# Layer 2 of a fused attention and two-layer kernel in units of 512 tokens instead of 384, with its buffers moved by 32 bytes

## The chip, the cores and the metric

The kernel runs on one core of one Trainium2 chip. The metric is the device time of one execution in microseconds (us). Three runs of the kernel before took 903.63, 903.86 and 904.91 us; the median is 903.86 us.

## The reference

Windowed attention over 4 x 8 heads, 576 positions and head size 64, then two layers over the 4 x 576 = 2304 tokens it leaves, each of width 512 with 2048 inner columns. Everything is fp32.

```python
def _moe_ref(x, w_in, w_out):          # layer 1
    h = np.maximum(x @ w_in, 0.0)
    return (h * h @ w_out)

def _moe2_ref(x, w_in, w_out):         # layer 2
    h = x @ w_in
    g = h * np.cos(h)
    return (g @ w_out)

x = attention(q, k, v)   # causal, window 64, softmax; regrouped to (2304, 512)
x = _moe_ref(x, ...)
return _moe2_ref(x, ...)
```

## The kernel before, in words

**Numbers.** Each fp32 operand of a layer's products is split into a high and a low fp32r part, and a product is three matmuls: high by high, and the two mixed ones. So one product of 128 contracted rows costs three LDWEIGHTS and three MATMULs.

**Work.** Both layers go through their tokens unit by unit, and within a unit through j = 0 to 15, 16 slices of 128 inner columns. One pair (unit, j) is called an item here. Its first product (function `g1`, matmuls at L833, tile `ph`) multiplies four 128-row chunks of w_in, the stationary operand, by the unit's X: 12 matmuls as wide as the unit has tokens. The activation follows on ScalarE (ACT) and VectorE (DVE). Its second product (`g2`) is added up over the 16 items in PSUM. In layer 1 (class `UnitA`, L624, tiles `accA`) w_out is stationary and the activations `g` move; units are 256 tokens three times and then 512 tokens three times, and the output goes through DRAM (`x2d`). In layer 2 (class `UnitB`, L766, tiles `accB`) the activations `gb` are stationary, 128 tokens at a time, and 512 columns of w_out move: three matmuls for each 128 tokens, whatever the unit's size. Layer 2 has six units of 384 tokens (`UB`), so an item is 12 matmuls of 384 columns and 9 of 512.

**Activation of layer 2** (`UnitB.act`): ACT `u` (L717), DVE rounding (L721), two DVE steps of range reduction (L725, L729) and a clamp (L732), ACT sine (L736), DVE product (L739), ACT copy to `gb` high (L743), DVE `gb` low (L746). All are as wide as the unit.

**Order.** A planner (`Plan.run`) writes out one list of instructions for each engine before anything runs. It goes by costs (`pe_us`, `act_us`, `dve_us`), by keys, and by rings that stand for the buffers; each engine then takes its list in that order. TensorE (PE) has a list laid down by `line`: in layer 2 `g1` of item i, then `g2` of item i-3.

**Buffers.** PSUM has four accumulators (`acc`), one for each 128 tokens of a layer-2 unit, and four tiles for `ph`. At a unit's end `UnitB.finish` copies each accumulator to one of the two `x2` tiles (L788, L790) and stores it (L794). The next unit's inputs come through the same two `x2` tiles (`UnitB.load`, L679, L683, L686). SBUF is filled from the left (X, the weights `W`, the layer-1 tiles `r`, `g`, `x2`) and, by pools opened with `side="right"`, from its right end: the attention's buffers, and after them the layer-2 pool `bp` with `u`, `r` and `gb`. In the built program every left-hand buffer named here starts at a multiple of 64 bytes (X at 17088, the weight slots from 49856 on, `g` at 193216 and 197312), and every buffer of the right end starts 32 bytes off one (`gb` at 217056, 220128, 223200, 226272; `qk` at 211296). The attention of the first two 256-token blocks is an exception: its second half (`guest`) lies in weight slots on the left.

Of the kernel before, what the change touches and what calls it, by code (L numbers as in the profile page):

```python
# [9 lines left out]
F32 = mybir.dt.float32  # L10
F32R = mybir.dt.float32r
# [17 lines left out]
def f32(ap):  # L29
    return ap.bitcast(F32)  # L30
# [55 lines left out]
class Plan:  # L86
# [80 lines left out]
def dve_us(n, fast=False):  # L167
    return 0.065 + n / (1920.0 if fast else 960.0)
# [4 lines left out]


def pe_us(n, passes=1):
    return max(0.107, 0.004 + passes * n / 2207.0)


@with_exitstack
def kernel(  # L180
# [53 lines left out]
    def dma(key, fn, nbytes, deps=(), take=(), use=(), n=1, order=()):  # L234
        return op({"SP": max(0.6 * n, nbytes / 360e3)}, key, fn, [*deps, *order], take, use, lat=2.2)
# [4 lines left out]
    def copy(e, o, i, scale=1.0):  # L240
        if e == "ACT":
            nc.scalar.activation(o, i, AF.Copy, scale=scale)  # L242
        elif e == "POOL":
            nc.gpsimd.tensor_scalar(o, i, scale, 1.0, ALU.mult, ALU.mult)
        elif scale == 1.0:
            nc.vector.tensor_copy(o, i)
        else:
            nc.vector.tensor_scalar(o, i, scale, None, ALU.mult)
# [408 lines left out]
                        x2_done[n, c] = o  # L657

    class UnitB:
        w = UB  # L660
        tiles = UB // P

        def __init__(self, n):
            self.n = n
            self.acc_b = [R["acc"].buf() for _ in range(self.tiles)]
            self.acc = {}
            self.xb = R["X"].buf()
            self.ready = {}

        def xt(self):  # L670
            return X[:, :, :, (2 * UA, 0)[self.xb.slot]:]

        def load(self, key, after, l=None):
            for c in range(NCC):
                t, b = {}, R["x2"].buf()

                def ld(e, c=c, t=t):
                    t["x"] = ma.tile([P, 512], F32, tag="x2", name=f"xr_{self.n}_{c}")
                    nc.sync.dma_start(  # L679
                        t["x"][:, 0:UB], x2d[:, c, self.n * UB:self.n * UB + UB])  # L680

                def hi(e, c=c, t=t):
                    copy(e, self.xt()[:, 0, c, 0:UB], t["x"][:, 0:UB])  # L683

                def lo(e, c=c, t=t):
                    nc.vector.tensor_tensor(  # L686
                        self.xt()[:, 1, c, 0:UB], t["x"][:, 0:UB], f32(self.xt()[:, 0, c, 0:UB]),
                        ALU.subtract)

                first, last = self.n * UB // UA, (self.n * UB + UB - 1) // UA  # L690
# [4 lines left out]
                l = dma(key + c, ld, P * UB * 4, deps, [b] + ([self.xb] if c == 0 else []),  # L695
                        [self.xb] if c else [])
                h = op({"DVE": dve_us(UB, True), "ACT": act_us(UB)}, key + c, hi, [l], use=[b, self.xb])
                o = op({"DVE": dve_us(UB)}, key + c, lo, [h], use=[b, self.xb])
                self.ready[c] = [h, o]
            return l  # L700

        def x(self, hl, c):
            return self.xt()[:, hl, c, 0:UB]

        def x_ready(self, c):
            return self.ready[c]
# [2 lines left out]
            return [self.xb]  # L709

        def act(self, ph, phb, nm, key, o_g1):
            ub, rb, gb = R["bu"].buf(), R["br"].buf(), R["bg"].buf()
            t = {}

            def e0(e):
                t["u"] = bp["b"].tile([P, UB], F32, tag="u", name=f"u_{nm}")
                nc.scalar.activation(  # L717
                    t["u"], ph()[:, 0:UB], AF.Identity, bias=quarter, scale=INV_2PI)

            def e1(e):  # L720
                nc.vector.tensor_scalar(t["u"], t["u"], MAGIC, MAGIC, ALU.add, ALU.subtract)  # L721

            def e2(e):
                t["r"] = bp["b"].tile([P, UB], F32, tag="r", name=f"rr_{nm}")
                nc.vector.scalar_tensor_tensor(  # L725
                    t["r"], t["u"], -C1, ph()[:, 0:UB], ALU.mult, ALU.add)

            def e3(e):
                nc.vector.scalar_tensor_tensor(t["r"], t["u"], -C2, t["r"], ALU.mult, ALU.add)  # L729

            def e4(e):
                nc.vector.tensor_scalar(  # L732
                    t["r"], t["r"], -PI_IN - HALF_PI, PI_IN - HALF_PI, ALU.max, ALU.min)

            def e5(e):
                nc.scalar.activation(t["u"], t["r"], AF.Sin, bias=hpi)  # L736

            def e6(e):
                nc.vector.tensor_tensor(t["r"], ph()[:, 0:UB], t["u"], ALU.mult)  # L739
# [8 lines left out]
            o = op({"ACT": act_us(UB, False)}, key, e0, [o_g1] + open_b, [ub], [phb])  # L748
            if sines:
                sines[-1].deps.append(o)  # L750
            o = op({"DVE": dve_us(UB, True)}, key, e1, [o], use=[ub])
            o = op({"DVE": dve_us(UB)}, key, e2, [o], [rb], [ub, phb])
            o = op({"DVE": dve_us(UB)}, key, e3, [o], use=[ub, rb])
            o = op({"DVE": dve_us(UB, True)}, key, e4, [o], use=[rb])
            o = op({"ACT": act_us(UB) + 0.1}, key, e5, [o], use=[ub, rb])
            sines.append(o)
            o = op({"DVE": dve_us(UB)}, key, e6, [o], use=[ub, rb, phb])
            h = op({"ACT": act_us(UB)}, key, e7, [o], [gb], [rb])
            l = op({"DVE": dve_us(UB)}, key, e8, [h], use=[rb, gb])
            return t, gb, [h, l]  # L760

        def g2(self, j, m, t, w):
# [7 lines left out]
        groups = UB // P  # L770
        group_us = 3 * pe_us(DM)

        def g2_bufs(self, j, m):
# [2 lines left out]
        def finish(self, key, o_last):  # L776
            for i in range(self.tiles):
                extra = self.n == NUB - 1 and i == self.tiles - 1
                t, b = {}, R["bg" if extra else "x2"].buf()

                def cp_(e, i=i, t=t, extra=extra):
                    if extra:
                        t["o"] = bp["b"].tile(
                            [P, 2 * UB], F32, tag="g", bufs=4, name=f"o_{self.n}_{i}")[:, 0:DM]
                    else:
                        t["o"] = ma.tile([P, DM], F32, tag="x2", name=f"o_{self.n}_{i}")
                    if e == "ACT":
                        nc.scalar.activation(t["o"], self.acc[i], AF.Copy)  # L788
                    else:
                        nc.vector.tensor_copy(t["o"], self.acc[i])  # L790

                def st(e, i=i, t=t):
                    r0 = self.n * UB + i * P
# [86 lines left out]
    for i in range(len(items) + LAG + 1):  # L880
# [95 lines left out]
```

## Time and profile before

| | |
|---|---|
| median of three runs | 903.86 us |
| the profiled execution | 904.37 us |
| its span, first to last instruction | 902.6 us |
| mean granted TensorE clock | 0.992 |
| PE busy | 879.0 us, 97% of the span |
| DVE busy / ACT busy | 563.3 us, 62% / 480.2 us, 53% |
| layer 2's products, first start to last | 489.58 us to 898.7 us |

The profile is of one execution, 0.51 us above the median of the runs. Its "busy" time of PE counts a matmul from its start to its modelled end; neighbouring matmuls overlap in it. The time that a matmul really takes from the stream is the distance from its start to the next one's start. In the timeline, the first column of a row is the start of a run of like instructions, the second the time from there to the end of the last of them.

### The profile page before, as it was taken

What the parts mean: (1) busy time and instruction counts of PE and PEld (TensorE: products, weight loads), DVE (VectorE), ACT (ScalarE), POOL (GpSimd) and SP (SyncE); (2) the same over time, 40 slices, a digit from 0 to 9 for tenths busy, and PEclk for the clock granted to TensorE, in tenths of its full rate; (3) what the DMA queues carried; (4) which work ended last, traced back from release to release, by engine and by line L of the source; (5) the groups of instructions that cost most, each with busy time, mean ns of one, the idle gap of its engine ahead of it and who ended that gap; (6) DMA issues with size and microseconds to landing.
All of it is one profiled execution on the core that took longest, in us unless ns stands there. A gap on an engine that the chain in (4) does not pass through costs nothing.

```text
span 902.6 us, 14462 instructions
## 1 busy us (share of the span) xinstructions
PE 879.0 (97%) x5616; PEld 776.9 (86%) x5616; DVE 563.3 (62%) x1295; ACT 480.2 (53%) x1019; POOL 5.0 (1%) x25
## 2 busy tenths in 40 slices
PE   5699999999999999999999999999999999999998
PEld 4599999998788878788888998998999999989987
DVE  4999956444455355443545966866866766766664
ACT  5989977666565565654433634433433443443333
POOL 2000000000000000000000000000000000000000
PEclk9799999999999999999999999999999999999999
DMA  7753235433533353224522200200200200200000
GB/s 317 303 227 129 75 120 177 161 133 112 183 120 125 137 180 132 94 97 135 200 94 93 82 1 1 72 1 1 71 0 1 71 1 1 71 1 1 36 0 36
DMA packets 23748, 85.47 MB, mean 95 GB/s; under 512 B 2432, under 2 KB 7040, under 8 KB 19584
## 3 DMA queue, kind: packets, MB, share of 16 engines
q1 hardware_dynamic: 23680, 84.55, 26.5%
q8 instruction: 44, 0.72, 0.3%
q14 instruction: 24, 0.20, 0.1%
HBM read 66.72 MB, written 17.83 MB: 94 GB/s over the span
## 4 chain that ended last, share of the span: by engine, by line
PE 91%; ACT 4%; DVE 3%; issue 1%; DMA 0%; ACTq 0%; DVEq 0%
PE ph L833 43%; PE accB L766 22%; PE accA L624 20%; PE S L468 2%; PE O L519 2%; PE T L505 2%; ACT raw_in_w_dram L242 1%; DVE cw_in_w_dram L298 1%; ACT pb L487 1%; DVE pb L481 0%; ACT g L601 0%; DVE pb L497 0%; ACT W_in_w_dram L242 0%; DMA qk<-in_qk_dram 0%; DVE W_in_w_dram L324 0%
## 5 line engine op out<-in xcount | busy, mean ns | idle before, releaser
L833 PE MATMUL ph<-X,W_in_w_dram 128*128 128x256 f32 (+1 forms) x1152 | 224.9, 343 | 1.3 <-DVE W_in_w_dram L324 1.3
L624 PE MATMUL accA<-g,W_in_w_dram 128*128 128x256 f32 (+1 forms) x1152 | 221.4, 338 | 0.0
L833 PE MATMUL ph<-X,W 128*128 128x384 f32 x1152 | 218.0, 337 | 0.0
L766 PE MATMUL accB<-W,gb 128*128 128x512 f32 x864 | 216.4, 395 | 0.0
L833 PEld LDWEIGHTS ph<-X,W 128*128 128x128 f32 x1152 | 205.2, 188 | 8.6
L833 PEld LDWEIGHTS ph<-X,W_in_w_dram 128*128 128x128 f32 x1152 | 182.1, 192 | 27.0 <-DVE W_in_w_dram L324 2.1
L624 PEld LDWEIGHTS accA<-g,W_in_w_dram 128*128 128x128 f32 x1152 | 179.9, 190 | 22.9 <-issue 0.5
L766 PEld LDWEIGHTS accB<-W,gb 128*128 128x128 f32 x864 | 161.0, 188 | 30.5
L717 ACT ACTIVATE u<-ph,quarter 128x384 f32<-128x384 f32 x96 | 55.8, 581 | 150.5 <-PE ph L833 150.5
L610 DVE TENSOR_TENSOR g<-r,g 128x256 fp32r<-128x256 f32 (+1 forms) x96 | 53.2, 555 | 89.8 <-ACT r L605 89.7
L721 DVE TENSOR_SCALAR u<-u 128x384 f32<-128x384 f32 x96 | 34.6, 360 | 109.1 <-ACT u L717 109.1
L743 ACT ACTIVATE gb<-rr 128x384 fp32r<-128x384 f32 x96 | 50.5, 526 | 84.9 <-DVE rr L739 84.2
L601 ACT ACTIVATE g<-r 128x256 fp32r<-128x256 f32 (+1 forms) x96 | 50.4, 525 | 76.2 <-PE accA L624 75.5
L597 ACT ACTIVATE r<-ph 128x256 f32<-128x256 f32 (+1 forms) x96 | 46.7, 486 | 56.8 <-PE ph L833 56.5
L242 ACT ACTIVATE raw_in_w_dram<-raw_in_w_dram 128x1024 f32<-128x1024 f32 x64 | 72.6, 1152 | 3.7 <-DMA raw_in_w_dram<-in_w_dram 2.5
L487 ACT ACTIVATE pb<-pb,mm 128x128 f32<-128x128 f32 x144 | 56.0, 392 | 17.9 <-DVE mm L481 17.8
L736 ACT ACTIVATE u<-rr,hpi 128x384 f32<-128x384 f32 x96 | 58.5, 610 | 1.3 <-DVE rr L732 1.3
L739 DVE TENSOR_TENSOR rr<-ph,u 128x384 f32<-128x384 f32 x96 | 52.9, 551 | 4.2 <-ACT u L736 3.6
L725 DVE SCALAR_TENSOR_TENSOR rr<-u,ph 128x384 f32<-128x384 f32 x96 | 53.1, 553 | 2.9
L746 DVE TENSOR_TENSOR gb<-rr,gb 128x384 fp32r<-128x384 f32 x96 | 53.0, 552 | 0.9 <-ACT gb L743 0.9
L729 DVE SCALAR_TENSOR_TENSOR rr<-u,rr 128x384 f32<-128x384 f32 x96 | 52.8, 550 | 0.7
L605 ACT ACTIVATE r<-r 128x256 f32<-128x256 f32 (+1 forms) x96 | 50.5, 526 | 3.0
(60 smaller groups left out, 547.1 us busy)
## 6 DMA issues: line engine op xcount, KB each, us to landing
raw_in_w_dram<-in_w_dram SPq DMA_DIRECT2D x32, 1024.0 KB, 7.5
qk<-in_qk_dram SPq DMA_DIRECT2D x18, 576.0 KB, 4.5
v<-in_v_dram SPq DMA_DIRECT2D x18, 512.0 KB, 3.7
w_dram<-cw_in_w_dram SPq DMA_DIRECT2D x16, 512.0 KB, 3.2
w<-w_dram SPq DMA_DIRECT2D x8, 1024.0 KB, 4.9
x_dram<-x SPq DMA_DIRECT2D x18, 256.0 KB, 2.6
xr<-x_dram SPq DMA_DIRECT2D x24, 192.0 KB, 2.4
out_dram<-o SPq DMA_DIRECT2D x18, 256.0 KB, 2.1
```

Source lines behind the costliest of these rows:

```text
L242: nc.scalar.activation(o, i, AF.Copy, scale=scale)
L487: nc.scalar.activation(t["pb"][:, e, r, i], t["pb"][:, e, r, i], AF.Exp, bias=t["mm"][:, e, r, i:i + 1], scale=-1.0, accum_out=t["sm"][:, ...
L610: nc.vector.tensor_tensor(t["g"][:, 1], t["r"], f32(t["g"][:, 0]), ALU.subtract)
L624: nc.tensor.matmul(self.acc[i][:, k, :], w[:, 1, wl, m * P:m * P + P], t["g"][:, gl, :], start=(j == 0 and p == 0 and k == 0), stop=(j == ...
L717: nc.scalar.activation(t["u"], ph()[:, 0:UB], AF.Identity, bias=quarter, scale=INV_2PI)
L725: nc.vector.scalar_tensor_tensor(t["r"], t["u"], -C1, ph()[:, 0:UB], ALU.mult, ALU.add)
L729: nc.vector.scalar_tensor_tensor(t["r"], t["u"], -C2, t["r"], ALU.mult, ALU.add)
L736: nc.scalar.activation(t["u"], t["r"], AF.Sin, bias=hpi)
L739: nc.vector.tensor_tensor(t["r"], ph()[:, 0:UB], t["u"], ALU.mult)
L746: nc.vector.tensor_tensor(t["g"][:, 1], t["r"], f32(t["g"][:, 0]), ALU.subtract)
L766: nc.tensor.matmul(self.acc[m], t["g"][:, gl, m * P:m * P + P], w[:, 1, wl], start=(j == 0 and k == 0), stop=(j == NJ - 1 and k == 2))
L833: nc.tensor.matmul(t["ph"][:, 0:u.w], wb.tile[:, 0, wl, c * P:c * P + P], u.x(xl, c), start=(c == 0 and k == 0), stop=(c == NCC - 1 and k ...
```

## The change

Layer 2 goes in units of 512, 512, 512, 512 and 256 tokens (`UB = 512`, the last unit takes what is left). A full item is 12 matmuls of 512 columns at the first product and 12 of 512 at the second; an item of the last unit is 12 of 256 and 6 of 512.

The tile `u` is no longer in the layer-2 pool but in layer 1's tile `r`; `gb` is in layer 1's `g` for items of even number, and in the layer-2 pool (two buffers instead of four) for odd ones. A tile of 8 floats (32 bytes) is placed at the right end of SBUF before everything else there; the built program then has every right-hand buffer at a multiple of 64 (`gb` at 193216, 197312, 221120, 225216; `qk` at 211264). The planner's cost of a matmul goes from 0.004 us + n/2207 to 0.0134 us + n/2400. The load of layer 2's first unit now also depends on the last store of layer 1's next to last unit. An SBUF slot of X holds 512 columns where 384 were used.

```diff
 def pe_us(n, passes=1):
-    return max(0.107, 0.004 + passes * n / 2207.0)
+    return max(0.108, 0.0134 + passes * n / 2400.0)
...
-    UB = 384
+    UB = 512
...
-    NUB = NT // UB
+    NUB = -(-NT // UB)
...
+    edge = ctx.enter_context(tc.tile_pool(name="edge", bufs=1, side="right"))
+    edge.tile([P, 8], F32, name="edge")
     att = ExitStack()
...
-        "pb": Ring(1), "sm": Ring(2), "PT": Ring(1), "bu": Ring(2), "br": Ring(2), "bg": Ring(4), "X": Ring(2),
+        "pb": Ring(1), "sm": Ring(2), "PT": Ring(1), "br": Ring(2), "bg": Ring(2), "X": Ring(2),
...
         def __init__(self, n):
-            self.n = n
+            self.n, self.t0 = n, n * UB
+            self.w = min(UB, NT - self.t0)
+            self.tiles = self.groups = self.w // P
...
         def act(self, ph, phb, nm, key, o_g1):
-            ub, rb, gb = R["bu"].buf(), R["br"].buf(), R["bg"].buf()
+            w = self.w
+            old = int(nm) % 2 == 0
+            ub, rb, gb = R["r"].buf(), R["br"].buf(), R["g" if old else "bg"].buf()
...
-                t["u"] = bp["b"].tile([P, UB], F32, tag="u", name=f"u_{nm}")
+                t["u"] = ma.tile([P, 512], F32, tag="r", name=f"u_{nm}")[:, 0:w]
...
-                t["g"] = bp["b"].tile([P, 2, UB], F32R, tag="g", bufs=4, name=f"gb_{nm}")
+                t["g"] = (ma if old else bp["b"]).tile(
+                    [P, 2, UB], F32R, tag="g", name=f"gb_{nm}")[:, :, 0:w]
...
         if i == NA:
-            loaded = units[NSA].load(pos - 6, [])
+            loaded = units[NSA].load(pos - 6, [x2_done[NUA - 3, NCC - 1]])
```

The other lines of the diff put `w`, the width of the unit, where `UB` stood.

PE's list at the end of layer 2's first unit, before; `accB_0_5087` to `accB_2_5101` are the first unit's accumulators, `accB_0_5659` the second unit's first, and x3 or x12 counts like matmuls in a row:

```order
L833 MATMUL ph_5604<-X,W_2_4597 128x384 x12
L766 MATMUL accB_0_5087<-W_15_5046,gb_5568 128x512 x3
L766 MATMUL accB_1_5095<-W_15_5046,gb_5568 128x512 x3
L766 MATMUL accB_2_5101<-W_15_5046,gb_5568 128x512 x3
L833 MATMUL ph_5640<-X,W_3_4636 128x384 x12
L766 MATMUL accB_0_5659<-W_0_4495,gb_5602 128x512 x3
L766 MATMUL accB_1_5668<-W_0_4495,gb_5602 128x512 x3
```

The same place now, `accB_0_5092` to `accB_3_5112` being the first unit's accumulators and `accB_0_5714` the second unit's first:

```order
L837 MATMUL ph_5654<-X,W_2_4601 128x512 x12
L771 MATMUL accB_0_5092<-W_15_5049,gb_5615 128x512 x3
L771 MATMUL accB_1_5099<-W_15_5049,gb_5615 128x512 x3
L771 MATMUL accB_2_5106<-W_15_5049,gb_5615 128x512 x3
L771 MATMUL accB_3_5112<-W_15_5049,gb_5615 128x512 x3
L837 MATMUL ph_5696<-X,W_3_4640 128x512 x12
L771 MATMUL accB_0_5714<-W_0_4483,gb_5652 128x512 x3
L771 MATMUL accB_1_5723<-W_0_4483,gb_5652 128x512 x3
```

The sequence is the same; the first product is wider, and there are four accumulators to a unit where there were three, so that the new unit's first one is the old unit's first one, and none of the four stands free between them.

ACT's list at the same unit's end, before (`o_1` is the second output tile of the unit; its first and third are copied by DVE):

```order
L736 ACTIVATE u_5588<-rr_5595,hpi 128x384
L788 ACTIVATE o_1_5635<-accB_1_5095 128x512
L743 ACTIVATE gb_5644<-rr_5595 128x384
L717 ACTIVATE u_5663<-ph_5640,quarter 128x384
L736 ACTIVATE u_5622<-rr_5638,hpi 128x384
```

The same place now (`o_1` to `o_3` are output tiles two to four; DVE copies the first):

```order
L740 ACTIVATE u_5635<-rr_5642,hpi 128x512
L792 ACTIVATE o_1_5684<-accB_1_5099 128x512
L748 ACTIVATE gb_5693<-rr_5642 128x512
L792 ACTIVATE o_2_5712<-accB_2_5106 128x512
L792 ACTIVATE o_3_5719<-accB_3_5112 128x512
L721 ACTIVATE u_5721<-ph_5696,quarter 128x512
L740 ACTIVATE u_5672<-rr_5691,hpi 128x512
```

Two more copies stand on ACT ahead of the next `u`, and each of them needs an `x2` tile that the store of an earlier output has left.

SP's list where layer 2's first unit is loaded, before (`xr` are the loads, `x_5` the stores of layer 1's unit of tokens 1280 to 1791):

```order
L679 DMA xr_0_4350<-x_dram 128x384
L679 DMA xr_1_4367<-x_dram 128x384
L679 DMA xr_2_4391<-x_dram 128x384
L340 DMA w_0_4403<-w_dram 128x2x1024
L316 DMA w_dram<-cw_in_w_dram_4375 128x1024
L679 DMA xr_3_4433<-x_dram 128x384
L649 DMA x_dram<-x_5_0_4438 128x512
L649 DMA x_dram<-x_5_1_4459 128x512
```

The same place now:

```order
L652 DMA x_dram<-x_5_2_4454 128x512
L652 DMA x_dram<-x_5_3_4460 128x512
L681 DMA xr_0_4490<-x_dram 128x512
L681 DMA xr_1_4512<-x_dram 128x512
L681 DMA xr_2_4534<-x_dram 128x512
L343 DMA w_1_4541<-w_dram 128x2x1024
L681 DMA xr_3_4563<-x_dram 128x512
```

The four loads have moved from ahead of the four `x_5` stores to behind them. On all engines the lists of attention and layer 1 also differ here and there from about 115 us on, by instructions of neighbouring tasks that have changed places.

## Rows read from the trace of the kernel before

**Rows 1.** The page: busy time by engine, share of the span.
```profile
PE 879.0 (97%) x5616; PEld 776.9 (86%) x5616; DVE 563.3 (62%) x1295; ACT 480.2 (53%) x1019; POOL 5.0 (1%) x25
PE 91%; ACT 4%; DVE 3%; issue 1%; DMA 0%; ACTq 0%; DVEq 0%
```

**Rows 2.** Stretches: busy us of each engine (x instructions), clock, DMA share, GB/s.
```profile
130.00:160.00 30.00, 29.96 (x337) 28.70 (x336) 19.99 (x62) 21.96 (x66) 0.00 (x0) 1.00 0.51 167
200.00:489.00 289.00, 288.76 (x1743) 235.87 (x1742) 134.23 (x307) 155.19 (x326) 0.00 (x0) 1.00 0.40 136
489.60:899.00 409.40, 409.40 (x2041) 369.11 (x2039) 283.11 (x625) 168.43 (x312) 0.00 (x0) 1.00 0.07 23
```

**Rows 3.** Timeline of PE, layer 1, units of 512 (start us, us, instruction, count).
```profile
451.50 2.88 PE L833 MATMUL ph<-X,W_in_w_dram 128*128 128x512 f32 x12
454.22 2.88 PE L624 MATMUL accA<-g,W_in_w_dram 128*128 128x512 f32 x12
456.94 2.88 PE L833 MATMUL ph<-X,W_in_w_dram 128*128 128x512 f32 x12
```

**Rows 4.** Timeline of PE, layer 1, units of 256 followed by 512.
```profile
200.33 1.60 PE L624 MATMUL accA<-g,W_in_w_dram 128*128 128x256 f32 x12
201.77 2.91 PE L833 MATMUL ph<-X,W_in_w_dram 128*128 128x512 f32 x12
204.52 1.60 PE L624 MATMUL accA<-g,W_in_w_dram 128*128 128x256 f32 x12
205.95 2.91 PE L833 MATMUL ph<-X,W_in_w_dram 128*128 128x512 f32 x12
```

**Rows 5.** Timeline, all engines, one item of layer 2.
```profile
867.37 2.27 PE L833 MATMUL ph<-X,W 128*128 128x384 f32 x12
...
869.48 2.26 PE L766 MATMUL accB<-W,gb 128*128 128x512 f32 x9
...
871.58 1.75 PE L833 MATMUL ph<-X,W 128*128 128x384 f32 x9
```

**Rows 6.** Timeline of PE where layer 1 runs into layer 2.
```profile
489.58 2.27 PE L833 MATMUL ph<-X,W 128*128 128x384 f32 x12
491.69 2.92 PE L624 MATMUL accA<-g,W_in_w_dram 128*128 128x512 f32 x12
494.45 2.27 PE L833 MATMUL ph<-X,W 128*128 128x384 f32 x12
496.55 2.92 PE L624 MATMUL accA<-g,W_in_w_dram 128*128 128x512 f32 x12
499.31 0.87 PE L833 MATMUL ph<-X,W 128*128 128x384 f32 x4
```

**Rows 7.** Timeline, all engines, the last items of layer 2.
```profile
890.51 8.56 PE L766 MATMUL accB<-W,gb 128*128 128x512 f32 x36
890.77 0.58 ACT L717 ACTIVATE u<-ph,quarter 128x384 f32<-128x384 f32 x1 [1.61 <-PE ph L833]
...
895.50 0.56 DVE L746 TENSOR_TENSOR gb<-rr,gb 128x384 fp32r<-128x384 f32 x1 [0.59 <-ACT gb L743]
```

**Rows 8.** Groups by line and form: busy us, mean ns | idle before.
```profile
L766 PE MATMUL accB<-W,gb 128*128 128x512 f32 x864 | 216.4, 395 | 0.0
L721 DVE TENSOR_SCALAR u<-u 128x384 f32<-128x384 f32 x96 | 34.6, 360 | 109.1 <-ACT u L717 109.1
L610 DVE TENSOR_TENSOR g<-r,g 128x512 fp32r<-128x512 f32 x48 | 33.1, 690 | 70.3 <-ACT r L605 70.3
L605 ACT ACTIVATE r<-r 128x512 f32<-128x512 f32 x48 | 30.4, 633 | 1.5
L610 DVE TENSOR_TENSOR g<-r,g 128x256 fp32r<-128x256 f32 x48 | 20.1, 421 | 19.5 <-ACT r L605 19.5
L605 ACT ACTIVATE r<-r 128x256 f32<-128x256 f32 x48 | 20.1, 419 | 1.5
```

**Rows 9.** Timeline of PE, attention scores: buffers at the right end, then on the left.
```profile
16.80 1.99 PE L468 MATMUL S<-qk 64*64 64x128 f32 x32
...
33.97 1.99 PE L468 MATMUL S<-qk 64*64 64x128 f32 x32
```

**Rows 10.** Output tiles of layer 2, from the view of tile o.
```profile
L790 DVE COPY o<-accB x10: 683/684/691, 567.8 to 839.8; 128x512 f32<-128x512 f32 x10
L788 ACT ACTIVATE o<-accB x8: 597/599/599, 568.2 to 899.1; 128x512 f32<-128x512 f32 x8
DMA to landing us min/median/max: 2.0/2.1/3.9
```

**Rows 11.** Timeline of SP's DMA issues before layer 2.
```profile
389.30 11.05 SPq L679 DMA_DIRECT2D xr<-x_dram  x3
...
411.96 6.36 SPq L649 DMA_DIRECT2D x_dram<-x  x4
```

More of the change, by code (lines that the diff above doesn't have):

```diff
@@ L659 @@
     class UnitB:
-        w = UB
-        tiles = UB // P
         def __init__(self, n):
-            self.n = n
+            self.n, self.t0 = n, n * UB
+            self.w = min(UB, NT - self.t0)
+            self.tiles = self.groups = self.w // P
             self.acc_b = [R["acc"].buf() for _ in range(self.tiles)]
@@ L670, in xt @@
         def xt(self):
-            return X[:, :, :, (2 * UA, 0)[self.xb.slot]:]
+            return X[:, :, :, (2 * UA, 0)[self.xb.slot]:][:, :, :, 0:self.w]
         def load(self, key, after, l=None):
@@ L679, in ld @@
                     nc.sync.dma_start(
-                        t["x"][:, 0:UB], x2d[:, c, self.n * UB:self.n * UB + UB])
+                        t["x"][:, 0:self.w], x2d[:, c, self.t0:self.t0 + self.w])
                 def hi(e, c=c, t=t):
-                    copy(e, self.xt()[:, 0, c, 0:UB], t["x"][:, 0:UB])
+                    copy(e, self.xt()[:, 0, c], t["x"][:, 0:self.w])
                 def lo(e, c=c, t=t):
                     nc.vector.tensor_tensor(
-                        self.xt()[:, 1, c, 0:UB], t["x"][:, 0:UB], f32(self.xt()[:, 0, c, 0:UB]),
+                        self.xt()[:, 1, c], t["x"][:, 0:self.w], f32(self.xt()[:, 0, c]),
                         ALU.subtract)
-                first, last = self.n * UB // UA, (self.n * UB + UB - 1) // UA
+                first, last = self.t0 // UA, (self.t0 + self.w - 1) // UA
                 deps = [l] + [x2_done[u, c] for u in range(first, last + 1)]
@@ L694, in load @@
                     deps.append(g1_last[(NUA - 3, NUA - 1)[self.n]])
-                l = dma(key + c, ld, P * UB * 4, deps, [b] + ([self.xb] if c == 0 else []),
+                l = dma(key + c, ld, P * self.w * 4, deps, [b] + ([self.xb] if c == 0 else []),
                         [self.xb] if c else [])
-                h = op({"DVE": dve_us(UB, True), "ACT": act_us(UB)}, key + c, hi, [l], use=[b, self.xb])
-                o = op({"DVE": dve_us(UB)}, key + c, lo, [h], use=[b, self.xb])
+                h = op({"DVE": dve_us(self.w, True), "ACT": act_us(self.w)}, key + c, hi, [l], use=[b, self.xb])
+                o = op({"DVE": dve_us(self.w)}, key + c, lo, [h], use=[b, self.xb])
                 self.ready[c] = [h, o]
@@ L702, in x @@
         def x(self, hl, c):
-            return self.xt()[:, hl, c, 0:UB]
+            return self.xt()[:, hl, c]
         def x_ready(self, c):
@@ L723, in e2 @@
             def e2(e):
-                t["r"] = bp["b"].tile([P, UB], F32, tag="r", name=f"rr_{nm}")
+                t["r"] = bp["b"].tile([P, UB], F32, tag="r", name=f"rr_{nm}")[:, 0:w]
                 nc.vector.scalar_tensor_tensor(
-                    t["r"], t["u"], -C1, ph()[:, 0:UB], ALU.mult, ALU.add)
+                    t["r"], t["u"], -C1, ph()[:, 0:w], ALU.mult, ALU.add)
             def e3(e):
@@ L738, in e6 @@
             def e6(e):
-                nc.vector.tensor_tensor(t["r"], ph()[:, 0:UB], t["u"], ALU.mult)
+                nc.vector.tensor_tensor(t["r"], ph()[:, 0:w], t["u"], ALU.mult)
             def e7(e):
-                t["g"] = bp["b"].tile([P, 2, UB], F32R, tag="g", bufs=4, name=f"gb_{nm}")
+                t["g"] = (ma if old else bp["b"]).tile(
+                    [P, 2, UB], F32R, tag="g", name=f"gb_{nm}")[:, :, 0:w]
                 nc.scalar.activation(t["g"][:, 0], t["r"], AF.Copy)
@@ L746, in e8 @@
                 nc.vector.tensor_tensor(t["g"][:, 1], t["r"], f32(t["g"][:, 0]), ALU.subtract)
-            o = op({"ACT": act_us(UB, False)}, key, e0, [o_g1] + open_b, [ub], [phb])
+            o = op({"ACT": act_us(w, False)}, key, e0, [o_g1] + open_b, [ub], [phb])
             if sines:
                 sines[-1].deps.append(o)
[L751 to L755, printed above, removed]
+            o = op({"DVE": dve_us(w, True)}, key, e1, [o], use=[ub])
+            o = op({"DVE": dve_us(w)}, key, e2, [o], [rb], [ub, phb])
+            o = op({"DVE": dve_us(w)}, key, e3, [o], use=[ub, rb])
+            o = op({"DVE": dve_us(w, True)}, key, e4, [o], use=[rb])
+            o = op({"ACT": act_us(w) + 0.1}, key, e5, [o], use=[ub, rb])
             sines.append(o)
-            o = op({"DVE": dve_us(UB)}, key, e6, [o], use=[ub, rb, phb])
-            h = op({"ACT": act_us(UB)}, key, e7, [o], [gb], [rb])
-            l = op({"DVE": dve_us(UB)}, key, e8, [h], use=[rb, gb])
+            o = op({"DVE": dve_us(w)}, key, e6, [o], use=[ub, rb, phb])
+            h = op({"ACT": act_us(w)}, key, e7, [o], [gb], [rb])
+            l = op({"DVE": dve_us(w)}, key, e8, [h], use=[rb, gb])
             return t, gb, [h, l]
@@ L783, in cp_ @@
                         t["o"] = bp["b"].tile(
-                            [P, 2 * UB], F32, tag="g", bufs=4, name=f"o_{self.n}_{i}")[:, 0:DM]
+                            [P, 2 * UB], F32, tag="g", name=f"o_{self.n}_{i}")[:, 0:DM]
                     else:
@@ L792, in st @@
                 def st(e, i=i, t=t):
-                    r0 = self.n * UB + i * P
+                    r0 = self.t0 + i * P
                     nc.sync.dma_start(out[r0:r0 + P, :], t["o"])
```

3 lines of the change are left out of this document (1 added, 2 removed).

## The prediction

> **What bounds the kernel now.** I read the page first: PE is busy 97% of the span and holds 91% of the chain that ended last [rows 1]. The table of stretches says where that is no average: from 200 us on PE is hardly ever idle (288.76 of 289.00 us, then 409.40 of 409.40 us), at the full granted clock of 1.00, while DVE is busy 283 of the last 409 us and ACT 168 [rows 2]. So layer 2, 45% of the span, takes as long as PE's stream of matmuls takes, and a change there is worth what it takes out of that stream, as long as the others keep up.
>
> What one matmul takes is read from distances between starts. In layer 1, 12 matmuls of 512 columns go from 451.50 to 454.22 us and the next 12 to 456.94: 2.72 us, or 226.7 ns each [rows 3]. Twelve of 256 columns take 201.77 - 200.33 = 1.44 us, 120 ns each [rows 4]. The difference, 106.7 ns for 256 columns, is 0.4167 ns a column (2.4 GHz), and what is left over is 226.7 - 213.3 = 13.4 ns a matmul. A matmul of 384 columns would then take 160 + 13.4 = 173.4 ns.
>
> Layer 2 does not reach that. Its item is 12 matmuls of 384 from 867.37 to 869.48 us and 9 of 512 from there to 871.58: 2.11 and 2.10 us [rows 5], where 12 x 173.4 ns is 2.08 and 9 x 226.7 ns is 2.04. The first is 0.03 us too long, the second 0.06. There are two kinds of excess in this. One comes with each change of width: where 384-column products alternate with layer 1's 512-column ones, whose operands lie elsewhere, the 512-column dozen takes 494.45 - 491.69 = 2.76 us instead of 2.72 and the 384-column one 2.11 [rows 6]; where 256 and 512 alternate, the 512 dozen takes 204.52 - 201.77 = 2.75 and the 256 dozen 1.43, in sum 0.02 too long [rows 4]. The other stays: the last 36 second products run alone, with nothing of another width between them, and take 8.56 us to the end of the last. Less the 0.395 us of that last one [rows 7, 8] that is 8.165 / 35 = 233.3 ns each, 6.6 ns above the 226.7 of layer 1. DVE and ACT have finished their activation work by 896.06 us [rows 7], so they aren't what slows the rest of it. What the second product of layer 2 has for itself is its stationary operand, `gb`, the only one of the layers' operands that lies 32 bytes off a multiple of 64.
>
> **The change part by part.** Layer 2's stream before: from 489.58 us [rows 6] to the end of the 36, 890.51 + 36 x 0.2333 = 898.91 us [rows 7], is 409.33 us; two dozens of layer 1 in it take 2.76 us each [rows 6]; 403.8 us are left (96 items of 4.21 us would be 404.2).
>
> Fewer, wider first products: 4 x 16 items with 12 of 512 columns and 16 with 12 of 256, 960 matmuls where there were 1152, over the same 442,368 columns. 192 x 13.4 ns = 2.6 us less.
>
> The Trainium skill (TensorE: Matmul & The Clock Gate, Back-to-back issue gap) gives about 2.5 ns a matmul beyond its columns at the full clock. Here the two widths give 13.4 ns, so this rule and the trace differ; by the rule the saving would be 0.5 us and the time 2.1 us later than mine. The measurement decides.
>
> No change of width in the four large units: both products are 512 wide, as in [rows 3], so the 0.03 us in each first product goes: 96 x 0.03 = 2.9 us. In the last unit's 16 items 0.02 us each comes back, 0.3 us [rows 4].
>
> `gb` at multiples of 64: second products at 226.7 instead of 233.3 ns, 864 x 6.6 ns = 5.7 us. This is the uncertain term. The trace has no second product with the other address. From below it is 0 (the 6.6 ns belong to something else), from above all of 6.6 ns, the level of [rows 3]; a gain below layer 1's steady level is excluded, since columns and clock are the same there, and a loss too, since the operand moves to an address of the kind all other layer operands have. I take the upper end: same width, same clock, same weight size, other operands at 64.
>
> Sum of the stream after: 64 x 24 x 0.2267 = 348.2 us and 16 x (1.44 + 6 x 0.2267 + 0.02) = 45.1 us, 393.3 in all, 10.5 less than 403.8. The two layer-1 dozens among them lose their excess too, 0.1.
>
> The end: before, the last item's activation starts 0.26 us after the trailing run of 36 and its `gb` is ready at 896.06, 5.55 us after 890.51, where 27 matmuls (6.3 us) stand ahead of its own [rows 7]. Now 18 x 0.2267 = 4.08 us stand ahead. With 256 tokens a full-rate DVE step is (690 - 421)/2 = 0.13 us shorter than at 384, an ACT step 0.11 [rows 8], four and three of these, and two fast DVE steps at half: 1.0 us in all, so ready after 4.55 us. PE waits 0.5 us.
>
> DVE and ACT in the wide items: a DVE step at 512 takes 0.69 us [rows 8], four of these and two fast ones at about 0.43 (0.36 at 384 [rows 8], at half the slope) are 3.6 us in an item of 5.44, 67%, where 283 of 409 us are 69% [rows 2]. Three items lie between a first product and its second, 16 us, against a chain of 5.3 us at 384 [rows 7] and about 6.3 at 512.
>
> The loads of layer 2's first unit move behind the `x_5` stores on SP. Before, three of them were issued from 389.30 us and the stores from 411.96 to 418.32 [rows 11]; issued after 418 they have 70 us until PE wants them at 489.58 [rows 6]. Nothing; if that cover were gone, PE would wait for it once. The planner's new matmul costs reorder attention and layer 1 from 115 us on. PE waits 0.04 us of 130 to 160 and 0.24 of 200 to 489 [rows 2], so nothing is to be gained and a badly placed copy could cost up to about 1 us; I take 0. Attention's buffers move to multiples of 64 as well: its score matmuls take 1.99 us at the right end and 1.99 in the weight slots on the left, which are at 64 [rows 9]. Nothing.
>
> Sum: 904.37 - 10.5 - 0.1 + 0.5 = 894.3 us for an execution like the profiled one, which stood 0.5 above the median of the runs: **893.8 us**.
>
> **The rivals.**
>
> *A, the forecast*: both excesses go. 893.8, with 892.3 to 896 for the reordering, the end and a stray wait.
>
> *B, the address does nothing*: the 6.6 ns belong to the roles in this product (activations stationary, weights moving). For it: the scores do not care about the address [rows 9], though they are small. Against: layer 1 has the same forms with the roles turned and settles at 226.7 [rows 3]. Then 864 x 0.2333 = 201.6 us, and first products that follow a slower product start off their level as in [rows 4], 64 x 2.75 + 16 x 1.44 = 199.0: 400.6, a gain of 3.2, less 0.5 at the end. 901.2 us.
>
> The Trainium skill speaks for B: in SBUF — State Buffer, Door 1: The DMA port swizzle, it has engine reads go by 16-byte lines, and 32 bytes off a multiple of 64 is still a whole number of these. No run here has yet set one address against the other for this operand.
>
> *D, half of it*: the steady 6.6 ns goes only where `gb` lies on the left in layer 1's `g`, or some wait takes 2 to 5 us: 896 to 899.5.
>
> *C, slower*: four accumulators for four tiles. At the ends of the four large units the next unit's first product leaves 2.72 us before its second needs the old accumulators. The third copy needs an `x2` tile from the first store. With T the start of the old unit's last second product: its first accumulator is done at T + 0.68, copied by DVE in 0.68 [rows 10] after a step or two, at about T + 2.2, landed 2.1 later, third copy until T + 5.0; it is wanted at T + 2 x 2.72 + 1.36 = T + 6.8. 1.8 us to spare, and 0 with the longest landing of 3.9 [rows 10]. To lose the 10 us, each of the four ends would have to be late by 2.5 us more: a landing of 6.4 us. ACT's `u` and `gb` stand behind those copies, but with three items of lead. 905 or more.
>
> **How the numbers follow.** A 0.76, D 0.06, B 0.14, C 0.04. The median of another set of runs can be told from no change at about 0.2% (1.8 us). Faster holds A, D and B, less some 0.02 for a B with stalls: 0.94; same 0.02; slower 0.04. The range runs from A's lower end, with some room for attention's order, to the near side of B: 891.8 to 901.0.
>
> **What would show it.** Second products at 226.7 ns from start to start, alone at the end and within a unit (12 in 2.72 us): A; at 233: B; two levels by turns of items: D. First products 12 in 2.72 us in the large units. A wait of about 0.5 us before the last item's second product. PE idle at the large units' ends, with ACT's `o` waiting for the store: C. The stretch from layer 2's first matmul to its last near 399 us instead of 409. The forecast is wrong if layer 1 ends more than 1 us from where it did, or if the second product keeps 233 ns.

## The result, and the profile after

The changed kernel takes 894.62 us in the median of four runs (893.62 to 894.97), against 903.97 for the kernel before in the same comparison; the ratio of the runs is 0.989, with a 95% interval of 0.9878 to 0.9903. It is 1.1% faster, and the forecast of 893.8 us lies 0.8 below it.

The profiled execution took 894.97 us with a span of 893.2. First two stretches, with the columns of [rows 2], whose first and last row they answer to.

```profile
130.00:160.00 30.00, 28.88 (x328) 27.73 (x328) 18.91 (x51) 20.94 (x58) 0.00 (x0) 1.00 0.47 159
486.00:889.00 403.00, 403.00 (x1868) 337.04 (x1867) 267.95 (x516) 162.35 (x272) 0.00 (x0) 1.00 0.08 25
```

PE is again busy throughout layer 2, at the full clock; but 1.1 us are idle at 130 to 160 us, where it was 0.04. The view of PE's waits (who for whom, us in total, times, longest) names the place; before, the same row read 1.1, once. Of the two waits the one ahead of 130 us stands in both kernels: PE is busy 28.81 us from 100 to 130 us, where it was 28.86. The other is new.

```profile
PE O L522 <- ACT PT L245: 2.3, 2, 1.2
```

The timeline of PE, answering to [rows 6] (the run from layer 1 into layer 2), [rows 5] (items of a large unit), and [rows 4] (widths 256 and 512 by turns, where the last unit begins):

```profile
490.35 2.88 PE L837 MATMUL ph<-X,W 128*128 128x512 f32 x12
493.07 2.88 PE L627 MATMUL accA<-g,W_in_w_dram 128*128 128x512 f32 x12
...
604.59 2.88 PE L771 MATMUL accB<-W,gb 128*128 128x512 f32 x12
607.31 2.88 PE L837 MATMUL ph<-X,W 128*128 128x512 f32 x12
610.03 2.88 PE L771 MATMUL accB<-W,gb 128*128 128x512 f32 x12
...
837.22 2.91 PE L771 MATMUL accB<-W,gb 128*128 128x512 f32 x12
839.97 1.59 PE L837 MATMUL ph<-X,W 128*128 128x256 f32 x12
841.40 2.91 PE L771 MATMUL accB<-W,gb 128*128 128x512 f32 x12
```

Every dozen of 512 columns takes 2.72 us, 226.7 ns a matmul, first and second product alike. Where the last unit's 256-column first products stand between the second products of the unit before, a dozen of these takes 2.75 and a dozen of the first products 1.43, as layer 1 had it at its own change of width. The last items (all engines):

```profile
883.60 5.68 PE L771 MATMUL accB<-W,gb 128*128 128x512 f32 x24
...
887.15 0.42 ACT L748 ACTIVATE gb<-rr 128x256 fp32r<-128x256 f32 x1 [0.49 <-DVE rr L743]
887.60 0.42 DVE L751 TENSOR_TENSOR gb<-rr,gb 128x256 fp32r<-128x256 f32 x1 [0.48 <-ACT gb L748]
```

24 matmuls take 5.68 us to the end of the last, 5.29 to its start, against 23 x 0.2267 = 5.21: under 0.1 us of waiting and change of width together. The view of the output tiles (idle time of the copying engine, what ended it), answering to [rows 10]:

```profile
  DMA out_dram<-o: 4.0, 4
DMA to landing us min/median/max: 2.0/2.0/2.7
```

So ACT and DVE did wait for stores at the four large units' ends, 4.0 us in all, and PE shows no idle time there.

The sum, by the first matmul of layer 2 and the start of its last one: 398.5 us (490.35 to 888.9) where it was 409.1 (489.58 to 898.7). That is 10.6 us less. Layer 2 began 0.8 us later, and what follows the last matmul's start, to the span's end, is 4.3 us long and was 3.9. 10.6 - 0.8 - 0.4 = 9.4 us, the difference of the two spans and of the two executions.

### The profile page after: what moved, and what is told of

It reads as the page before. It is cut to its first block, busy times and chain, and to the rows that moved or that the text cites. A ratio compares the mean times of both kernels' runs of the same rounds, so it can differ in the third digit from the quotient of the medians.

```text
span 893.2 us, 13884 instructions
## 1 busy us (share of the span) xinstructions
PE 867.7 (97%) x5424; PEld 741.5 (83%) x5424; DVE 546.0 (61%) x1182; ACT 474.8 (53%) x980; POOL 5.0 (1%) x25
## 4 chain that ended last, share of the span: by engine, by line
PE 91%; DVE 4%; ACT 3%; DMA 1%; issue 1%; SPq 0%; ACTq 0%; DVEq 0%
PE ph L837 42%; PE accB L771 22%; PE accA L627 20%; PE S L471 2%; PE O L522 2%; PE T L508 2%; ACT raw_in_w_dram L245 1%; DMA raw_in_w_dram<-in_w_dram 1%; DVE cw_in_w_dram L301 1%; DVE W_in_w_dram L327 1%; DVE pb L484 0%; DVE pb L500 0%; ACT W_in_w_dram L245 0%; DMA qk<-in_qk_dram 0%; ACT g L604 0%
## 5 line engine op out<-in xcount | busy, mean ns | idle before, releaser
L837 PE MATMUL ph<-X,W 128*128 128x512 f32 (+1 forms) x960 | 209.8, 368 | 0.0
L837 PEld LDWEIGHTS ph<-X,W 128*128 128x128 f32 x960 | 169.3, 188 | 31.2
L721 ACT ACTIVATE u<-ph,quarter 128x512 f32<-128x512 f32 (+1 forms) x80 | 51.7, 646 | 148.8 <-PE ph L837 148.8
L725 DVE TENSOR_SCALAR u<-u 128x512 f32<-128x512 f32 (+1 forms) x80 | 32.0, 400 | 121.2 <-ACT u L721 121.2
L748 ACT ACTIVATE gb<-rr 128x512 fp32r<-128x512 f32 (+1 forms) x80 | 47.2, 590 | 83.6 <-DVE rr L743 83.6
L740 ACT ACTIVATE u<-rr,hpi 128x512 f32<-128x512 f32 (+1 forms) x80 | 53.7, 672 | 0.3 <-DVE rr L736 0.2
L729 DVE SCALAR_TENSOR_TENSOR rr<-u,ph 128x512 f32<-128x512 f32 (+1 forms) x80 | 50.7, 634 | 2.5
L743 DVE TENSOR_TENSOR rr<-ph,u 128x512 f32<-128x512 f32 (+1 forms) x80 | 50.4, 630 | 1.4 <-ACT u L740 1.3
L751 DVE TENSOR_TENSOR gb<-rr,gb 128x512 fp32r<-128x512 f32 (+1 forms) x80 | 50.5, 631 | 1.0 <-ACT gb L748 1.0
L733 DVE SCALAR_TENSOR_TENSOR rr<-u,rr 128x512 f32<-128x512 f32 (+1 forms) x80 | 50.4, 630 | 0.3
```

The source lines that it names most:

```text
L721: nc.scalar.activation(t["u"], ph()[:, 0:w], AF.Identity, bias=quarter, scale=INV_2PI)
L729: nc.vector.scalar_tensor_tensor(t["r"], t["u"], -C1, ph()[:, 0:w], ALU.mult, ALU.add)
L837: nc.tensor.matmul(t["ph"][:, 0:u.w], wb.tile[:, 0, wl, c * P:c * P + P], u.x(xl, c), start=(c == 0 and k == 0), stop=(c == NCC - 1 and k ...
```

## The experiments

Each kernel ran beside the kernel before on the same chip. "Layer 2" is the time from the start of its first matmul to the start of its last one in the profile of the run; two dozens of layer 1 lie in it in every kernel. In experiments 1 to 5 all engines have the same lists, in the same order, as in the kernel that the edit was made to; only addresses differ.

**1. The sizes alone, and the addresses alone.** First the sizes, with all of `gb` (and layer 1's `r`, `g` and `x2`) 32 bytes off a multiple of 64:

```diff
-    edge = ctx.enter_context(tc.tile_pool(name="edge", bufs=1, side="right"))
-    edge.tile([P, 8], F32, name="edge")
+    gap = ctx.enter_context(tc.tile_pool(name="gap", bufs=1))      # ahead of the pool ma
+    gap.tile([P, 8], F32, name="gap")
```

> The changed kernel with every gb buffer moved 32 bytes off a multiple of 64 (the 32-byte tile at the right end left out, a 32-byte gap ahead of layer 1's r and g); units of 512 as in the change, weights and X where they were. Theory S (a stationary operand of 128 fp32 columns that starts 32 bytes off a multiple of 64 costs 6.6 ns a matmul): second products of layer 2 at 233.3 ns, 864 x 6.6 = 5.7 us, and first products that start off their level after them, 64 x 0.03 = 1.9 us: 894.6 + 7.6 = about 902. Rival R (the excess belonged to the changes of width alone, and went with 512 beside 512): second products at 226.7 ns, 894.6 us.

902.87 us (901.2 to 904.35), 0.998 of the kernel before (0.9969 to 0.999). Layer 2 takes 404.2 us. Its PE timeline, and then its matmuls by line (count, shortest, median and longest ns, first and last start):

```profile
601.51 2.96 PE L771 MATMUL accB<-W,gb 128*128 128x512 f32 x12
604.31 2.89 PE L837 MATMUL ph<-X,W 128*128 128x512 f32 x12
607.04 2.96 PE L771 MATMUL accB<-W,gb 128*128 128x512 f32 x12
609.83 2.43 PE L837 MATMUL ph<-X,W 128*128 128x512 f32 x10
```

```profile
L837 PE MATMUL ph<-X,W x960: 278/389/402, 491.0 to 889.7; 128*128 128x512 f32 x154, 128*128 128x256 f32 x38
L771 PE MATMUL accB<-W,gb x864: 389/395/398, 507.6 to 895.1; 128*128 128x512 f32 x173
```

A dozen second products takes 2.79 to 2.80 us (233 ns each), with no other width beside it: rival R falls. The first products after them take 2.73, nearly their level at once; the 1.9 us expected there did not come. That the time is near the expected 902 us all the same is luck. The edit moves layer 1's `g` too, and with it layer 1's second products slow down, in which the weights are stationary and `g` moves:

```profile
443.67 2.97 PE L627 MATMUL accA<-g,W_in_w_dram 128*128 128x512 f32 x12
446.48 2.92 PE L837 MATMUL ph<-X,W_in_w_dram 128*128 128x512 f32 x12
```

2.81 us a dozen, where layer 1 had 2.72 [rows 3]; theory S, which speaks of the stationary operand alone, has no place for that. It is one reason why the time shows less than the 4.9 us that layer 2 gained. In the profiled execution (901.2 us, the fastest of nine) layer 2 begins 1.4 us later than before, and 0.4 us more follow its last matmul's start, so that 3.2 us are left.

Then the addresses alone, the kernel before with the two lines of `edge`:

> The kernel before, units of 384, with the 32-byte tile at the right end alone. Theory S: the trailing 36 second products alone settle to 226.7 ns instead of 233.3; within an item the change of width keeps the second products high for their first nine, as layer 1's after 384-column ones (230 to 231 ns on average, where 233 stood), so only about 0.015 us an item and 0.2 at the end: 904.0 - 1.6 = about 902.4. Rival R: nothing changes, 904.0, and the trailing 36 stay at 233.3 ns.

903.0 us (901.68 to 905.48), 0.9992 of the kernel before (0.9981 to 1.0003): by its time, nothing that can be told. Layer 2 takes 407.1 us (492.7 to 899.8) instead of 409.1. The timeline within it and at its end:

```profile
600.80 2.27 PE L835 MATMUL ph<-X,W 128*128 128x384 f32 x12
602.91 2.24 PE L768 MATMUL accB<-W,gb 128*128 128x512 f32 x9
...
891.79 8.36 PE L768 MATMUL accB<-W,gb 128*128 128x512 f32 x36
```

The 36 at the end take 8.36 us instead of 8.56 [rows 7]: less 0.39 for the last, 7.97 / 35 = 227.7 ns, the first few still high. Within an item the nine take 2.24 us to the end of the last, where it was 2.26 [rows 5]: coming after 384-column matmuls, they have hardly settled before the next change of width. The profiled execution is the slowest of ten, 905.48 us: layer 2 begins 3.1 us later in it than before, 2.6 us of that by a wait that experiment 6 looks at. So the two parts are worth more together than apart: in layer 2, sizes alone 4.9 us, addresses alone 2.0, both 10.6.

**2. Half of the items off.**

```diff
-    edge = ctx.enter_context(tc.tile_pool(name="edge", bufs=1, side="right"))
-    edge.tile([P, 8], F32, name="edge")
```

> The changed kernel without the 32-byte tile at the right end: gb of odd items 32 bytes off a multiple of 64, gb of even items at one. Theory S: two levels by turns, 12 second products in 2.72 us for even items and 2.80 for odd ones, first products after odd items 0.03 us longer: 432 x 6.6 ns + 32 x 0.03 = 3.8 us, 898.4 us. Rival R: one level of 226.7 ns, 894.6 us.

895.69 us (895.67 to 897.84). Two levels by turns, as theory S said:

```profile
603.40 2.88 PE L769 MATMUL accB<-W,gb 128*128 128x512 f32 x12
606.12 2.89 PE L835 MATMUL ph<-X,W 128*128 128x512 f32 x12
608.85 2.96 PE L769 MATMUL accB<-W,gb 128*128 128x512 f32 x12
611.64 0.62 PE L835 MATMUL ph<-X,W 128*128 128x512 f32 x2
```

2.72 us and then 2.79. Layer 2 takes 401.2 us (488.4 to 889.6), 2.7 more than in the changed kernel; 432 matmuls x 6.6 ns would be 2.9. The whole is 2.7 us below the expected 898.4: the 1.0 us in first products did not come here either, and layer 2 began 1.9 us sooner than in the profile of the changed kernel.

**3. Which operand.** The weights moved (a gap of 32 bytes ahead of their slots and another behind), and X moved (one ahead of X, one behind). In both, what lies further right moves by the two gaps, 64 bytes: layer 1's `g` with `gb` of even items, and in the second run the weights too; `gb` of odd items stays. So it is not X "alone" that moves, as the expectation has it.

```diff
+    gap = ctx.enter_context(tc.tile_pool(name="gap", bufs=1))      # run 1: ahead of wp
+    gap.tile([P, 8], F32, name="gap")
...
+    cp.tile([P, 8], F32, name="gap")                               # run 2: ahead of X
     X = cp.tile([P, 2, NCC, 4 * UA], F32R, name="X")
+    cp.tile([P, 8], F32, name="gap2")
```

> The changed kernel with the weight slots moved 32 bytes off a multiple of 64; gb, g and X stay at multiples. Theory S (what costs 6.6 ns is a stationary operand off a multiple of 64): all matmuls with weights as the stationary operand slow down, layer 1's 1152 of 512 columns and layer 2's 768 to 233.3 ns (1920 x 6.6 = 12.7 us), and if the cost is the same beside 256 columns another 1344 x 6.6 = 8.9 us; the second products of layer 2, where the weights move, stay at 226.7: 894.6 + 12.7 to 21.6 = 907 to 916 us. Rival M (either operand): the second products of layer 2 are at 233 as well, 5.7 us more. Rival L (only the buffers at the right end or the roles of layer 2's second product matter): 894.6 us.

908.55 us (907.6 to 909.46), 1.0049 of the kernel before (1.0028 to 1.0071). All products of both layers are slower, the second products of layer 2 too, where the weights move and `gb` is where it was (odd items) or 64 bytes further (even items), at a multiple of 64 in either case:

```profile
440.61 2.96 PE L631 MATMUL accA<-g,W_in_w_dram 128*128 128x512 f32 x12
443.41 2.96 PE L841 MATMUL ph<-X,W_in_w_dram 128*128 128x512 f32 x12
446.21 2.96 PE L631 MATMUL accA<-g,W_in_w_dram 128*128 128x512 f32 x12
...
605.69 2.96 PE L775 MATMUL accB<-W,gb 128*128 128x512 f32 x12
608.49 2.96 PE L841 MATMUL ph<-X,W 128*128 128x512 f32 x12
```

2.80 us a dozen everywhere. Theory S, which excepted those second products, falls. The time alone would not show it, since 908.55 lies in the range that theory S gave.

> The changed kernel with X alone moved 32 bytes off a multiple of 64, the moving operand of both layers' first products. Theory S: no matmul changes, 12 first products of 512 columns in 2.72 us, 894.6 us. Rival M (either operand): first products at 233 ns, 2112 x 6.6 = 13.9 us, about 908 us.

902.13 us (901.53 to 905.3). X is the moving operand, and the first products of both layers are slow:

```profile
441.48 2.96 PE L839 MATMUL ph<-X,W_in_w_dram 128*128 128x512 f32 x12
444.28 2.91 PE L629 MATMUL accA<-g,W_in_w_dram 128*128 128x512 f32 x12
...
602.17 2.91 PE L773 MATMUL accB<-W,gb 128*128 128x512 f32 x12
604.92 2.96 PE L839 MATMUL ph<-X,W 128*128 128x512 f32 x12
607.71 2.89 PE L773 MATMUL accB<-W,gb 128*128 128x512 f32 x12
```

2.80 and 2.79 us a dozen of first products. It isn't the stationary operand as such; either one will do. The second products of the odd item at 602.17 us, whose operands are now 64 bytes apart, take 2.75 us. Both runs came out below the expected time of rival M (913 us at the least for the first, about 908 for the second), since 256-column matmuls behave otherwise (last section). An estimate for the first: 2784 matmuls of 512 columns at 6.6 ns more and 1344 of 256 columns at 3 ns less are 14.4 us; it is 13.9 us above the changed kernel's 894.62.

**4. How far off.** The right end moved by 96 bytes, which puts `gb` of odd items at a multiple of 128, and `gb` of odd items 16 bytes into a larger tile:

```diff
-    edge.tile([P, 8], F32, name="edge")
+    edge.tile([P, 24], F32, name="edge")                           # run 1
...
+                    bp["b"].tile([P, 2, UB + 16], F32R, tag="g", name=f"gb_{nm}")[:, :, 4:4 + w])   # run 2
```

> The changed kernel with 96 bytes instead of 32 at the right end: gb of odd items at a multiple of 128, where every other operand lies 64 off one. If multiples of 64 are all that counts: 226.7 ns throughout, 894.6 us. If the distance between operands or multiples of 128 count, odd and even items differ.

894.75 us (two runs). Not one level: odd items take 2.74 us, even ones 2.72.

```profile
603.25 2.88 PE L771 MATMUL accB<-W,gb 128*128 128x512 f32 x12
605.97 2.88 PE L837 MATMUL ph<-X,W 128*128 128x512 f32 x12
608.69 2.91 PE L771 MATMUL accB<-W,gb 128*128 128x512 f32 x12
611.43 2.88 PE L837 MATMUL ph<-X,W 128*128 128x512 f32 x12
```

The difference is small, but it stands in the whole trace: from start to start the median is 229 ns for odd items and 227 for even ones. A multiple of 128, the "better" address if anything, is slower here than 64 off one. What sets these operands apart is that the weights lie 64 off. This points at the distance between the two operands, which experiment 5 tests.

> The changed kernel with gb of odd items 16 bytes off a multiple of 64. Theory S with blocks of 64 bytes: odd items' second products at 233 ns or above, as with 32 bytes off, about 896 us. If only multiples of 16 counted (lines of 16 bytes): 226.7 ns throughout, 894.6 us.

896.54 us (two runs); odd items take 2.79 us with 16 bytes too. In the larger tile the low part of `gb` starts 64 bytes further off than the high part, so of three matmuls two have their operands 16 bytes apart modulo 128, and the third 80; from start to start the trace has medians of 231 to 234 ns for both kinds.

```profile
609.97 2.95 PE L772 MATMUL accB<-W,gb 128*128 128x512 f32 x12
612.76 2.90 PE L838 MATMUL ph<-X,W 128*128 128x512 f32 x12
```

**5. Everything off by the same 32 bytes.** In all kernels so far, one operand of the slow products lay off and the other not. Here X, weights, `g`, `gb` and attention's buffers are all 32 bytes off a multiple of 64:

```diff
-    edge = ctx.enter_context(tc.tile_pool(name="edge", bufs=1, side="right"))
-    edge.tile([P, 8], F32, name="edge")
+    cp.tile([P, 8], F32, name="gap")
     X = cp.tile([P, 2, NCC, 4 * UA], F32R, name="X")
```

> The changed kernel with every operand of TensorE 32 bytes off a multiple of 64: X, weights, g, gb and attention's buffers, so that stationary and moving operand stand to each other as in the changed kernel. Theory Q (what counts is how far the two operands of the stream lie apart, modulo 64 or 128 bytes; so far every kernel with one operand off had the two 16 or 32 bytes apart): 226.7 ns throughout, the same time as the changed kernel. Theory S' (an operand off a multiple of 64 costs, stationary or moving): no matmul of either layer at 226.7, at least the 14 us of the kernel with the weights moved, about 908 or more.

893.99 us (893.56 to 894.33), beside 893.49 for the changed kernel on the same chip. Theory Q holds and S' falls:

```profile
440.49 2.88 PE L836 MATMUL ph<-X,W_in_w_dram 128*128 128x512 f32 x12
443.21 2.88 PE L626 MATMUL accA<-g,W_in_w_dram 128*128 128x512 f32 x12
...
603.69 2.88 PE L770 MATMUL accB<-W,gb 128*128 128x512 f32 x12
606.41 2.88 PE L836 MATMUL ph<-X,W 128*128 128x512 f32 x12
```

2.72 us a dozen in both layers, with none of their operands at a multiple of 64.

**6. The planner's costs, and the later load.**

```diff
-    return max(0.108, 0.0134 + passes * n / 2400.0)      # runs 1 and 2
+    return max(0.107, 0.004 + passes * n / 2207.0)
...
-            loaded = units[NSA].load(pos - 6, [x2_done[NUA - 3, NCC - 1]])     # run 3
+            loaded = units[NSA].load(pos - 6, [])
```

> The changed kernel with the planner's matmul cost of before (0.004 + n/2207). If the new costs placed PE's wait for a copy of attention at 130 to 160 us (1.1 us idle there instead of 0.04), it goes: layer 2 starts at 489.6 us instead of 490.3 and the time is 893.9. If the wider units or the later load of layer 2's first unit did it, the lists of layer 1 stay as changed and the time is 894.6.

> The changed kernel with the planner's matmul cost of before, beside the changed kernel on the same chip. If the planner's new cost matters: 0.3 to 0.8 us less than the changed kernel. If what layer 1 lost in the profile was a wait that comes and goes: the same time within 0.3 us.

> The changed kernel once more, beside the others on the same chip: 894.6 us, PE waits for ACT's PT copies at 130 to 160 us between 0 and 1.2 us, from execution to execution.

With the old costs 894.27 us (893.76 to 896.39) and, in another comparison, 894.23 (893.5 to 894.69), in which the changed kernel took 893.49 (892.49 to 894.71). No gain from the old costs. PE's wait for `PT` is 1.1 and 1.2 us in the two profiles with the old costs and 2.3 and 2.5 in two of the changed kernel, but anything from 1.1 to 2.9 in the eight other kernels that keep the new costs, seven of them with the very lists of the changed kernel. So it varies where costs and lists do not. That it comes and goes in one and the same kernel, as was expected, is not shown: the two executions of the changed kernel are alike. What brings it on stays open.

> The changed kernel without the new dependency of the load of layer 2's first unit. Theory W (the old place of that load holds an x2 tile in the middle of layer 1's fifth unit's end, behind a 1 MB load, so that an output copy waits for a store and PE for the copy: 0.1 us in the profile before, 2.6 us in the one with the 32 bytes alone): PE waits at layer 1's accA at about 420 us again, 0.1 to 2.6 us, and the median is 0 to 2.6 us above the changed kernel's. Rival (the load's place costs nothing, as forecast): the same time.

894.50 us (893.3 to 895.1) against 893.49 (892.49 to 894.71): 1.0 us apart in the direction of theory W, but the ranges overlap. The wait itself is there in the profile. The timeline of all engines at the end of layer 1's fifth unit:

```profile
407.32 0.37 SPq L343 DMA_DIRECT2D w<-w_dram  x1
...
408.98 0.32 SPq L681 DMA_DIRECT2D xr<-x_dram  x1
...
414.94 0.43 DVE L249 CAST X<-xr 128x512 fp32r<-128x512 f32 x1 [4.70 <-DMA xr<-x_dram]
...
418.29 0.60 ACT L647 ACTIVATE x<-accA 128x512 f32<-128x512 f32 x1 [1.38 <-DMA x_dram<-x]
418.94 0.96 PE L627 MATMUL accA<-g,W_in_w_dram 128*128 128x512 f32 x3 [0.55 <-ACT x L647]
```

The last of the four input loads is issued behind a load of weights and arrives late; DVE stands 4.70 us before it, the copies and stores of layer 1's outputs move back, and PE waits 0.55 us for an accumulator. In the timeline of the kernel before with only the addresses changed, PE's row at the same place reads

```profile
421.14 0.97 PE L626 MATMUL accA<-g,W_in_w_dram 128*128 128x512 f32 x3 [2.56 <-ACT x L646]
```

2.6 us. In the kernel before, the dozen of second products at 415.89 us takes 2.94 us to the next start instead of 2.72, so about 0.2 us went there. In the changed kernel's two profiles the dozens at that place take 2.72 us. That the time itself gains by the later load is not shown.

## Why the prediction was right, point by point

*What bounds the kernel.* Right: PE's stream is the time, and all of the gain is in layer 2.

*Fewer and wider first products, no change of width* (2.6 + 2.9 - 0.3 = 5.2 us). Right as a sum: the sizes alone took 4.9 us off layer 2, and near 5.1 without the two slower dozens of layer 1 that lie in it in that kernel. The two can't be told apart by these runs.

*`gb`, 5.7 us, the uncertain term.* Its size is right: from the sizes alone to the changed kernel layer 2 lost 404.2 - 398.5 = 5.7 us, 0.2 of that in the two dozens of layer 1. It is worth that only once the change of width is gone: with units of 384 the same move took 2.0 us, because the change of width holds second products near 231 ns by itself, which the step had as a cost of the first products alone. Its ground was not right. The step said that the operand "moves to an address of the kind all other layer operands have", as if a multiple of 64 were good in itself. A kernel with no operand at such a multiple is as fast, and one with `gb` at a multiple of 128 a little slower: what the change mended is the distance to the other operand. The bound "a loss is excluded" rested on the same ground and was luck in part: a `gb` at a multiple of 64 at another distance would have left some 2 ns.

*Attention's scores* [rows 9]: the reading was right, and the distance would account for it, though no run moved these operands apart. Both operands of a score matmul lie in one tile, `qk`, so their distance is the same wherever it lies. As evidence on the address, which rival B took from it, the row says nothing.

*Rival B* falls by 226.7 ns in the second products. The Trainium skill's rule beside it (SBUF — State Buffer, Door 1: The DMA port swizzle, lines of 16 bytes) does not describe this either: a start 16 or 32 bytes off is still a whole number of lines, and 16 bytes off cost about as much as 32.

*The Trainium skill's 2.5 ns a matmul* (TensorE: Matmul & The Clock Gate, Back-to-back issue gap): the Trainium skill gives this as the gap of a single matmul by itself, and about 131 ns a matmul for a stream of weight loads and matmuls of 512 columns. The prediction put the first in a stream's place. An estimate by it is 215.8 ns at 512 columns. The trace agrees with neither: the changed kernel has 226.7 ns throughout its large units, so that the 13.4 ns read from two widths held.

*Rival C.* The copies did wait for their stores, 4.0 us in four places, and PE had the slack that was worked out. *Rival D* did not happen in the changed kernel; it is what experiment 2 built.

*The end, 0.5 us:* mis-sized, under 0.1. The step counted from the low part of `gb`, but two of the first three matmuls need the high part alone, ready 0.45 us sooner, and the chain was 4.42 us long where 4.55 was forecast. Instead, what follows the last matmul's start grew by 0.4 us, from a cause that was not looked into. That this nearly makes up for the 0.5 us in the sum is luck.

*Layer 1's order, "nothing to be gained, up to about 1 us to lose, I take 0":* in the profiled execution layer 2 began 0.8 us later, and PE waited 1.2 us longer for copies of attention. These 0.8 us and the tail are the difference between 10.6 and the 9.4 us of the whole. With the same lists but other addresses that wait is shorter or longer (experiment 6).

*The load of layer 2's first unit, "Nothing":* right for the load, wrong for what it left. At its old place it took an output tile from layer 1 and could make PE wait, about 0.2 us before, 0.55 and 2.6 in two other profiles. The step looked only at who needs the loads, not at whose buffer they hold meanwhile.

No version here beats the changed kernel by more than can be told: 893.49 and 894.62 in its two comparisons, 893.99 to 894.27 for all operands moved together and for the old costs.

## What to carry to other kernels

Read a matmul's cost from the distance between starts, in a stretch where one width runs alone and in one where widths alternate, and compare like forms before deciding what a product costs: 233 ns in layer 2's second products beside 226.7 in layer 1's stood in the trace of the kernel before. Where one is slower without a wait, compare the addresses of its two operands with those of a form that isn't. And when a transfer is moved, ask whose buffer it held at its old place.

## What the runs showed of the hardware that was not expected

At 512 fp32r columns and a granted clock of 1.00, the time of a matmul in a stream goes with the distance in bytes between the start of its stationary and its moving operand: 226.7 ns where it is a multiple of 256, wherever the two lie, about 229 where it is 64 off a multiple of 128, about 233 where it is 32 or 16 off, whichever of the two is moved. No kernel here has the two exactly 128 bytes apart modulo 256, so whether the pattern repeats every 128 or every 256 bytes stays open. So does whether a matmul's own weights count or those of the next one: within a dozen both stand at the same distance, but for the kernel with 16 bytes. What in the chip does this the runs do not show.

At 256 columns the sign turns round. With the weights moved by 32 bytes the dozens of layer 1's 256-column second products go from one start to the next one's in 1.40 us, 117 ns, where 120 ns stood [rows 4]. The first two rows are of that kernel, the last is of the changed kernel, whose dozen takes 1.44 us to the next start at 188.65:

```profile
188.25 1.56 PE L631 MATMUL accA<-g,W_in_w_dram 128*128 128x256 f32 x12
189.65 1.57 PE L841 MATMUL ph<-X,W_in_w_dram 128*128 128x256 f32 x12
...
187.21 1.60 PE L627 MATMUL accA<-g,W_in_w_dram 128*128 128x256 f32 x12
```

So the kernel with the weights moved lost 13.9 us and not 18 or more.
